# Late attention's scores as products of float32 q and k, without their powers, sums, splits and float16 pairs

## The chip, the cores and the metric

The kernel runs on one core of a Trainium2 chip. The metric is the device time of one execution in microseconds (us), the median of three runs. Engines: PE (matrix products), PEld (its weight loads), DVE and POOL (vector), ACT (scalar), SP (which issues most DMA transfers). The inputs lie in DRAM as float32.

## The reference

Block-local attention over chunks of 64 positions (8 batches, 8 heads, 576 positions, head size 64), then a feed-forward network with `g = h - tanh(h)`:

```python
scores = scale * np.matmul(q_c, k_c.transpose(0, 1, 2, 4, 3))   # scale = 1/8, chunks of 64
scores = scores - np.max(scores, axis=-1, keepdims=True)
attn = np.exp(scores)
attn = attn / (np.sum(attn, axis=-1, keepdims=True) + 1e-09)
out = np.matmul(attn, v_c)
...
h = x @ w_in            # x: 4608 x 512, w_in: 512 x 2048
g = h - np.tanh(h)
return (g @ w_out).astype(np.float32)   # w_out: 2048 x 512
```

## The kernel before

**Groups.** The 4608 tokens are 36 pairs of 128; nine groups have four pairs (512 tokens) each. Groups 0 and 1 are *early*: their attention is in plain float32 (class `Early`, whose `products`, L183, does 16 float32 products of 64x64 a pair) while weights are still being loaded. Groups 2 to 8 are *late* (class `Late`): a group is done in two halves `b` of two pairs, in the shadow of the FFN of the group before. `FAST = 2` is the first of them.

**Late attention before the change.** q, k and v are loaded raw (L303: `xl<-qL`, `rawk<-kL`, `rawv<-vL`). For each of the three a power of two is wanted that brings it into float16's range: sums of magnitudes over a partition (q and k on ACT by `spread`, L107; v as a maximum on DVE in `halves`, L318) go to DRAM and come back on all partitions (`sent`, `returned`: the tiles `hop`, `all`), `greatest` and `scales` make the powers. `split` writes a float16 head on ACT (L341) and a float16 remainder on DVE (L342) for each half of q, k and v. `scores` then takes three terms (head by head, remainder by head, head by remainder), each of them 32 products of 64x64:

```python
for i, (a, b) in enumerate(((0, 0), (1, 0), (0, 1))):
    for e in range(2):
        for hp in range(4):
            for c, u in ((0, 0), (1, 1), (0, 1), (1, 0)):
```

Here `c` chooses the half of the rows and `u` the half of the columns of PE's array. Such a run of products of one line (L353) is called a burst below; the products of the attention's weights with v come in bursts of the same form, and these stay. The powers of q and k go into the scale of the exponential (`d["exp"]`, L370).

**The FFN.** Groups 0 and 1 use class `FeedForward` (first products L534 into PSUM tiles `ph`, activation L546/L543 to `t`, DVE L547/L544, then `gh` on ACT, L554, and `gl` on DVE, L555, second products L565 into `po`), group 0 with float32 weights in two parts (`wh`, `wl`). Groups 2 to 8 use class `Fast` (L617 and L657, all in float16). The first weights become float16 pairs between groups 0 and 1 (`convert`, L455 and L456 on ACT, L457 and L458 on DVE): `most` sums over the weights (L424 to L428 on DVE, then a reduction over partitions on POOL, L430), `power_of_two` (L114 to L116) gives `to_w`, and the first converted weight lies in the tile `first_place`.

**Order.** Up to the end of the first group's FFN a part of the work is put in order by the scheduler from the code's order and its own costs. From `with tc.manual_schedule()` on, the order is that of the code: `ahead` puts each step of late attention into a numbered slot of the FFN loop (16 units a group, two slots a unit). At the boundary between the two, the loads of group 2 and what comes just ahead of the manual part (`sums` of k, `halves` of v) are still placed by the scheduler, among the manual steps too. All DMA issues named here stand in SP's queue and are issued in its order.

Of the kernel before, what the change touches and what calls it, by code (L numbers as in the profile page):

```python
# [57 lines left out]
def attn_ffn_kernel(ctx: ExitStack, tc: tile.TileContext, qE, kE, vE, qL, kL, vL, w_in, w_out, out):  # L58
# [99 lines left out]
    class Early:  # L158
# [110 lines left out]
    class Late:  # L269
# [4 lines left out]
        def __init__(self, pool):  # L274
            self.pool, self.st = pool, defaultdict(dict)

            self.raw = {n: xpool.tile([P, KC, MOST], F32R, name="xl").bitcast(F32) if n == "q" else pool.tile([P, MOST // P, H * CH], F32, name=f"raw{n}", bufs=1) for n in "qkv"}
            self.q16 = self.v16 = None
            self.hop = ctx.enter_context(tc.tile_pool(name="hop", bufs=2, space=bass.MemoryType.DRAM))

        def sent(self, g):

            d = self.st[f"g{g}"]
            d["hop"] = self.hop.tile([P, 3], F32, name="hop")
            nc.sync.dma_start(out=d["hop"], in_=d["sums"])

        def returned(self, g):

            d = self.st[f"g{g}"]
            d["all"] = self.pool.tile([P, P, 3], F32, name="all", bufs=1)  # L290
            nc.sync.dma_start(out=d["all"].rearrange("p n c -> p (n c)"), in_=d["hop"].rearrange("p c -> (p c)").unsqueeze(0).broadcast_to([P, 3 * P]))

        def greatest(self, g):

            d = self.st[f"g{g}"]
            most = self.pool.tile([P, 3], F32, name="most", bufs=2)
            nc.vector.reduce_max(out=most, in_=d["all"].rearrange("p n c -> p c n"), axis=AX.X)
            self.scales(g, most)

        def load(self, p, i, some="qkv"):  # L300
# [4 lines left out]
        def sums(self, g, n, other):  # L305

            d = self.st[f"g{g}"]
            if "sums" not in d:
                d["sums"] = self.pool.tile([P, 3], F32, name="sums", bufs=2)
            spread(other.bitcast(U8).rearrange("p (a n) -> p a n", n=H * CH), self.raw[n], d["sums"][:, "qkv".index(n):"qkv".index(n) + 1])  # L310

        def halves(self, g, i):

            d = self.st[f"g{g}"]
            if i == 0:
                d["v"] = self.pool.tile([P, 2], F32, name="v", bufs=2)
            v = d["v"]
            nc.vector.tensor_reduce(out=v[:, i:i + 1], in_=self.raw["v"][:, 2 * i:2 * i + 2].rearrange("p i n -> p (i n)"), axis=AX.X, op=ALU.max, apply_absolute_value=True)  # L318
            if i:
                nc.vector.tensor_scalar(out=d["sums"][:, 2:3], in0=v[:, 0:1], scalar1=v[:, 1:2], scalar2=2.0 ** -12, op0=ALU.max, op1=ALU.mult)  # L320

        def scales(self, g, top):

            d = self.st[f"g{g}"]
            d["to"], d["from"] = (self.pool.tile([P, 3], F32, name=m, bufs=2) for m in ("to", "from"))
            power_of_two(top, d["to"], d["from"])
            d["exp"] = self.pool.tile([P, 1], F32, name="exp", bufs=2)
            nc.vector.scalar_tensor_tensor(out=d["exp"], in0=d["from"][:, 0:1], scalar=scale, in1=d["from"][:, 1:2], op0=ALU.mult, op1=ALU.mult)
            from_x[g], to_x[g] = d["from"][:, 2:3], d["to"][:, 2:3]

        def split(self, g, b, n):

            d, to = self.st[g, b], self.st[f"g{g}"]["to"][:, "qkv".index(n):"qkv".index(n) + 1]
            d["exp"] = self.st[f"g{g}"]["exp"]
            raw = self.raw[n][:, 2 * b:2 * b + 2].rearrange("p e n -> p (e n)")
            if n == "k":
                t = self.pool.tile([P, 2, 2 * H * CH], F16, name="a", bufs=1)
                hl = d["k"] = t[:, 0], t[:, 1]
            else:
                hl = self.q16 if n == "q" else self.v16  # L340
            nc.scalar.activation(hl[0], raw, AF.Copy, scale=to)  # L341
            nc.vector.scalar_tensor_tensor(out=hl[1], in0=raw, scalar=to, in1=hl[0], op0=ALU.mult, op1=ALU.subtract)  # L342

        def products(self, ps, stationary, moving):


            for i, (a, b) in enumerate(((0, 0), (1, 0), (0, 1))):
                for e in range(2):
                    for hp in range(4):
                        for c, u in ((0, 0), (1, 1), (0, 1), (1, 0)):  # L350
                            r = slice(c * CH, (c + 1) * CH)
                            first = i == e == hp == 0
                            nc.tensor.matmul(ps(c, e, hp)[u * D:(u + 1) * D], lhsT=stationary(a, r, e, hp, u), rhs=moving(b, r, e, hp, u), start=first, stop=(i == 2), skip_group_check=True)  # L353

        def scores(self, g, b):
            d = self.st[g, b]
            ps = d["ps"] = ps_a.tile([P, 2, 2, 4, CH], F32, name="psa")
            q, k = ([t.rearrange("p (e hp u n) -> p e hp u n", e=2, hp=4, u=2) for t in hl] for hl in (self.q16, d["k"]))
            self.products(lambda c, e, hp: ps[:, c, e, hp], lambda a, r, e, hp, u: q[a][r, e, hp, u], lambda b, r, e, hp, u: k[b][r, e, hp, u])

        def shifted(self, g, b):
            d = self.st[g, b]
# [4 lines left out]

        def exponent(self, g, b):
            d = self.st[g, b]
            nc.scalar.activation(d["s"], d["s"], AF.Exp, scale=d["exp"])  # L370

        def totals(self, g, b):
            d = self.st[g, b]
# [23 lines left out]
        def values(self, g, b, x):  # L397
            d = self.st.pop((g, b))
            xh, xl = x
            ps = ps_a.tile([P, 2, 4, 2, CH], F32, name="psa")  # L400
            v = [t.rearrange("p (e hp u n) -> p e hp u n", e=2, hp=4, u=2) for t in self.v16]
            self.products(lambda c, e, hp: ps[:, c, hp, e], lambda a, r, e, hp, u: v[a][r, e, hp, u], lambda b, r, e, hp, u: d["a16"][b][r, e, hp, u])
# [357 lines left out]
            store(nc.sync, 1, right)  # L760
            store(nc.scalar, 0, left)

    def sums(att, g, n):
        att.sums(g, n, ffn.tile([P, MOST], F32, name="t", bufs=3))

    def ahead(att, at, g):

        o = 2 * FC * (g - FAST)
# [2 lines left out]
            at[o + 2 * unit + part].append(lambda: f(*args))  # L771

        late = g == FAST
        later = g == FAST + 1
        put(1 + later, 0, sums, att, g, "q")
        if not late:
            put(2 + later, 0, sums, att, g, "k")
            put(0 if later else -3, later, att.halves, g, 0)
            put(2, not later, att.halves, g, 1)
        put(1 if late else 4, late, att.sent, g)  # L780
        put(2 if late else 4, not late, att.returned, g)
        put(4 if late else 5, -0.5 if late else 1, att.greatest, g)
        put(14 if late else 9, 1, lambda: powers.update({g: half.power_of(g)}))
        put(6, 0, lambda: xs.update({g: new_half_x()}))
        for b, u in enumerate((3, 13) if late else (6, 14)):
            put(u + late, -0.5 if late else 1, att.split, g, b, "q")
            spaced = late and not b
            put(u + 1 + spaced, -0.5 if spaced else 0, att.split, g, b, "k")
            other = u + 3 if spaced else u + 2 if late else u + 1
            put(other, -0.5 if spaced else 1, att.split, g, b, "v")  # L790
            if g + 1 < NG:
                for i in (2 * b, 2 * b + 1):
                    put(u + 1 + spaced, 1, att.load, FIRST[g + 1] + i, i, "qk")
                    put(other, 1, att.load, FIRST[g + 1] + i, i, "v")
            u += late
            put(u + 2, 0, att.scores, g, b)
# [174 lines left out]
        return [place_of("l", 0, fc, dtype) for fc in ORDER[some]]  # L971

    def for_attention():
        att.q16, att.v16 = places(slice(0, 2)), places(slice(2, 4))

    at[2].append(lambda: half.powers(1))
    def convert(i):
# [100 lines left out]
```

## Time and profile before

| | |
|---|---|
| time, median of 3 runs | 791.15 us (791.11 to 792.21) |
| span of the profiled execution | 789.5 us |
| PE busy | 780.6 us, 99% |
| DVE, ACT, POOL busy | 629.4, 467.7, 410.2 us |
| granted clock of PE, 216 to 776 us | 1.00 |

The time is measured around the whole execution, the span from its first to its last recorded instruction; the median lies 1.65 us above the span. The busy shares are averages over all stages. Line numbers in the rows are those of the kernel before.

### The profile page before, as it was taken

How to read it: one execution, taken by the hardware profiler on the slowest of the kernel's cores; microseconds unless marked ns; L12 is line 12 of the kernel's file. 1: busy time of each engine (PE TensorE's matmuls, PEld its weight loads, DVE VectorE, ACT ScalarE, POOL GpSimd, SP SyncE). 2: the span in 40 equal slices, each digit the busy share in tenths (PEclk: the TensorE clock that was granted, in tenths of full speed). 3: DMA queues.
4: the chain of work that ended last, by engine and by line, in shares of the span. 5: the costliest groups of instructions: out<-in, count | busy, mean ns of one | idle time of the engine just before them, and what ended most of it. 6: DMA issues, size and time to landing. Idle time of an engine off the chain costs nothing.

```text
span 789.5 us, 21247 instructions
## 1 busy us (share of the span) xinstructions
PE 780.6 (99%) x9096; PEld 658.7 (83%) x9099; DVE 629.4 (80%) x856; ACT 467.7 (59%) x714; POOL 410.2 (52%) x461
## 2 busy tenths in 40 slices
PE   8999999999999999999999999999999999999997
PEld 4878875666788888888888888888888888888887
DVE  5896998899899787878878687968796878686554
ACT  6887999667586456544654565546454645454332
POOL 1100003398876656565657456656556565656462
PEclk9999999999999999999999999999999999999999
DMA  9854442210232223222422132222322230302000
GB/s 349 320 188 159 161 161 63 81 28 15 67 91 83 54 82 60 87 54 59 78 43 90 30 98 48 82 49 74 65 83 56 81 64 3 54 2 54 2 27 27
DMA packets 61054, 64.62 MB, mean 82 GB/s; under 512 B 33952, under 2 KB 42016, under 8 KB 60960
## 3 DMA queue, kind: packets, MB, share of 16 engines
q1 hardware_dynamic: 60528, 62.61, 27.8%
q8 instruction: 71, 1.16, 0.6%
q10 hardware_dynamic: 432, 0.66, 0.2%
q14 instruction: 23, 0.19, 0.1%
HBM read 46.47 MB, written 9.45 MB: 71 GB/s over the span
## 4 chain that ended last, share of the span: by engine, by line
PE 94%; DVE 2%; DMA 1%; ACT 1%; issue 0%; POOL 0%; POOLq 0%; SPq 0%; ACTq 0%
PE ph L617 37%; PE po L657 32%; PE po L565 10%; PE ph L534 9%; PE psa L353 3%; PE po L732 1%; DMA raw<-w_out 1%; PE psa L183 1%; DMA k<-kE 1%; DVE wl L148 0%; PE psa L244 0%; ACT w L133 0%; ACT s L218 0%; DVE w L141 0%; DVE w L137 0%
## 5 line engine op out<-in xcount | busy, mean ns | idle before, releaser
L617 PE MATMUL ph<-xh,wh 128*128 128x256 f16 x2520 | 291.1, 273 | 0.0
L617 PEld LDWEIGHTS <-wh 128*128 128x128 f16 x2520 | 245.4, 98 | 29.2 <-issue 0.5
L626 POOL TENSOR_TENSOR xl<-xl 128x256 f32<-128x256 f32 x111 | 112.6, 1015 | 222.7 <-DVE xl L625 222.0
L624 ACT ACTIVATE t<-ph,sig 128x512 f32<-128x512 f32 x112 | 77.0, 687 | 216.2 <-PE ph L617 214.6
L625 DVE SCALAR_TENSOR_TENSOR xl<-ph,sig,t 128x512 f32<-128x512 f32 x112 | 83.5, 745 | 78.9 <-ACT t L624 78.8
L657 PEld LDWEIGHTS <-wl 128*128 128x128 f16 x1134 | 110.9, 98 | 12.9
L628 POOL TENSOR_TENSOR xl<-xl 128x256 f32<-128x256 f32 x111 | 103.9, 936 | 0.0
L627 POOL TENSOR_TENSOR xl<-xl 128x128 f32<-128x128 f32 x111 | 101.4, 913 | 0.0
L657 PE MATMUL po<-wl,wl 128*128 128x256 f16 x648 | 101.0, 273 | 0.0
L638 DVE SCALAR_TENSOR_TENSOR gl<-xl,to_g,gh 128x896 f16<-128x896 f32 x56 | 82.9, 1481 | 7.9 <-ACT gh L637 7.9
L657 PE MATMUL po<-wh,wl 128*128 128x256 f16 x486 | 85.5, 273 | 0.0
L638 DVE SCALAR_TENSOR_TENSOR wl<-xl,to_g,wl 128x896 f16<-128x896 f32 x56 | 71.1, 1269 | 16.6 <-ACT wl L637 15.1
L657 PEld LDWEIGHTS <-gh 128*128 128x128 f16 x756 | 73.0, 98 | 8.8
L637 ACT ACTIVATE wl<-xl,to_g 128x896 f16<-128x896 f32 x56 | 57.9, 1035 | 32.4 <-POOL xl L628 31.5
L657 PE MATMUL po<-wl,gh 128*128 128x256 f16 x544 | 74.7, 273 | 0.0
L534 PE MATMUL ph<-xh,wh 128*128 128x512 f16 (+2 forms) x252 | 59.3, 377 | 0.4 <-ACT xh L266 0.3
L637 ACT ACTIVATE gh<-xl,to_g 128x896 f16<-128x896 f32 x56 | 57.8, 1032 | 1.3 <-DVE from L115 0.6
L565 PE MATMUL po<-wh,gh 128*128 128x512 f32 x128 | 52.9, 416 | 0.0
L565 PE MATMUL po<-wl,gh 128*128 128x512 f32 x128 | 50.3, 395 | 0.2 <-POOL wl L148 0.2
L657 PE MATMUL po<-wl,gl 128*128 128x256 f16 x272 | 42.9, 273 | 0.0
L657 PEld LDWEIGHTS <-gl 128*128 128x128 f16 x378 | 37.0, 98 | 4.3
L657 PE MATMUL po<-wh,gh 128*128 128x256 f16 x212 | 36.3, 273 | 0.0
(185 smaller groups left out, 1236.9 us busy)
## 6 DMA issues: line engine op xcount, KB each, us to landing
raw<-w_in SPq DMA_DIRECT2D x16, 512.0 KB, 3.7
raw<-w_out SPq DMA_DIRECT2D x16, 512.0 KB, 5.1
xl<-qL SPq DMA_DIRECT2D x28, 256.0 KB, 3.2
rawk<-kL SPq DMA_DIRECT2D x28, 256.0 KB, 3.3
rawv<-vL SPq DMA_DIRECT2D x28, 256.0 KB, 3.4
out<-wl SPq DMA_DIRECT2D x55, 128.0 KB, 1.8
q<-qE SPq DMA_DIRECT2D x8, 256.0 KB, 5.7
v<-vE SPq DMA_DIRECT2D x8, 256.0 KB, 6.1
```

The costliest lines, as they stand in the source:

```text
L353: nc.tensor.matmul(ps(c, e, hp)[u * D:(u + 1) * D], lhsT=stationary(a, r, e, hp, u), rhs=moving(b, r, e, hp, u), start=first, stop=(i == 2 ...
L534: nc.tensor.matmul(ph, lhsT=w[:, kc * P:(kc + 1) * P], rhs=x[b][:, kc, cols], start=(k == 0), stop=(k == 3 * KC - 1))
L565: nc.tensor.matmul(self.po[t], lhsT=gg[a][:, ts], rhs=wt[fc][1][b], start=(fc == 0 and a == b == 0), stop=(fc == FC - 1 and a == 1))
L617: nc.tensor.matmul(self.ph[:, 1 - f::2, :], lhsT=half_w[fc][:, w, kc * P:(kc + 1) * P], rhs=rhs, start=(k == 0), stop=(k == 3 * KC - 1))
L624: nc.scalar.activation(t, self.ph, AF.Tanh, scale=sig)
L625: nc.vector.scalar_tensor_tensor(out=u[:, :4], in0=self.ph, scalar=sig, in1=t, op0=ALU.mult, op1=ALU.subtract)
L626: engine.tensor_add(u[:, 4:6], u[:, 1:3], u[:, 0:4:3])
L627: engine.tensor_add(u[:, 6], u[:, 1], u[:, 2])
L628: engine.tensor_sub(u[:, 0:4:3], u[:, 0:2], u[:, 2:4])
L637: nc.scalar.activation(gh, u, AF.Copy, scale=powers[1])
L638: nc.vector.scalar_tensor_tensor(out=gl, in0=u, scalar=powers[1], in1=gh, op0=ALU.mult, op1=ALU.subtract)
L657: nc.tensor.matmul(place[m], lhsT=part[:, self.SUM[m]], rhs=w[m][:, o], start=first, stop=(last and part is gl), skip_group_check=True)
```

## The change

The scores of late attention multiply q and k in float32, straight from the tiles into which they were loaded: one term of 32 products instead of three of 32. The sums and powers of q and k, their splits and their float16 places go. v keeps its power and its float16 pair; the hop through DRAM has one column. The steps of a group are put into other slots, the loads of q and k behind the scores that read the same tiles, and the first late group's loads are issued in the order v, k, q.

```diff
         def scales(self, g, top):
-            d = self.st[f"g{g}"]
-            d["to"], d["from"] = (self.pool.tile([P, 3], F32, name=m, bufs=2) for m in ("to", "from"))
-            power_of_two(top, d["to"], d["from"])
-            d["exp"] = self.pool.tile([P, 1], F32, name="exp", bufs=2)
-            nc.vector.scalar_tensor_tensor(out=d["exp"], in0=d["from"][:, 0:1], scalar=scale, in1=d["from"][:, 1:2], op0=ALU.mult, op1=ALU.mult)
-            from_x[g], to_x[g] = d["from"][:, 2:3], d["to"][:, 2:3]
...
+            to_x[g], from_x[g] = (self.pool.tile([P, 1], F32, name=m, bufs=2) for m in ("to", "from"))
+            power_of_two(top, to_x[g], from_x[g])
+
+        def split(self, g, b):
+
+            raw = self.raw["v"][:, 2 * b:2 * b + 2].rearrange("p e n -> p (e n)")
+            hi, lo = self.v16
+            nc.scalar.activation(hi, raw, AF.Copy, scale=to_x[g])
+            nc.vector.scalar_tensor_tensor(out=lo, in0=raw, scalar=to_x[g], in1=hi, op0=ALU.mult, op1=ALU.subtract)
+
+        def products(self, ps, stationary, moving, terms):
+
+
+            for i, (a, b) in enumerate(terms):
                 for e in range(2):
                     for hp in range(4):
                         for c, u in ((0, 0), (1, 1), (0, 1), (1, 0)):
                             r = slice(c * CH, (c + 1) * CH)
-                            first = i == e == hp == 0
-                            nc.tensor.matmul(ps(c, e, hp)[u * D:(u + 1) * D], lhsT=stationary(a, r, e, hp, u), rhs=moving(b, r, e, hp, u), start=first, stop=(i == 2), skip_group_check=True)
+                            first = len(terms) == 1 or i == e == hp == 0
+                            nc.tensor.matmul(ps(c, e, hp)[u * D:(u + 1) * D], lhsT=stationary(a, r, e, hp, u), rhs=moving(b, r, e, hp, u), start=first, stop=(i == len(terms) - 1), skip_group_check=True)
 
         def scores(self, g, b):
             d = self.st[g, b]
             ps = d["ps"] = ps_a.tile([P, 2, 2, 4, CH], F32, name="psa")
-            q, k = ([t.rearrange("p (e hp u n) -> p e hp u n", e=2, hp=4, u=2) for t in hl] for hl in (self.q16, d["k"]))
-            self.products(lambda c, e, hp: ps[:, c, e, hp], lambda a, r, e, hp, u: q[a][r, e, hp, u], lambda b, r, e, hp, u: k[b][r, e, hp, u])
+            q, k = (self.raw[n][:, 2 * b:2 * b + 2].rearrange("p e (hp u n) -> p e hp u n", hp=4, u=2) for n in "qk")
+            self.products(lambda c, e, hp: ps[:, c, e, hp], lambda a, r, e, hp, u: q[r, e, hp, u], lambda b, r, e, hp, u: k[r, e, hp, u], ((0, 0),))
...
-            nc.scalar.activation(d["s"], d["s"], AF.Exp, scale=d["exp"])
+            nc.scalar.activation(d["s"], d["s"], AF.Exp, scale=scale)
...
         late = g == FAST
-        later = g == FAST + 1
-        put(1 + later, 0, sums, att, g, "q")
         if not late:
-            put(2 + later, 0, sums, att, g, "k")
-            put(0 if later else -3, later, att.halves, g, 0)
-            put(2, not later, att.halves, g, 1)
-        put(1 if late else 4, late, att.sent, g)
-        put(2 if late else 4, not late, att.returned, g)
+            put(-3, 0, att.halves, g, 0)
+            put(1, 1, att.halves, g, 1)
+        put(1 if late else 2, late, att.sent, g)
+        put(2, not late, att.returned, g)
...
                 for i in (2 * b, 2 * b + 1):
-                    put(u + 1 + spaced, 1, att.load, FIRST[g + 1] + i, i, "qk")
+                    put(u + late + 2, 1, att.load, FIRST[g + 1] + i, i, "qk")
                     put(other, 1, att.load, FIRST[g + 1] + i, i, "v")
...
-    for n in "kvq":
+    for n in "vkq":
         for i in range(SIZES[FAST]):
             att.load(FIRST[FAST] + i, i, n)
-    sums(att, FAST, "k")
     for i in range(2):
         att.halves(FAST, i)
     with tc.manual_schedule():
```

The late products with v now pass their three terms as an argument; their code is otherwise the same. In the changed kernel's listings the line numbers are smaller by some 16: L353 is L337 there, L534 L518, L547 L531, L555 L539, L554 L538, L565 L549, L318 L312, L427 L411, L455 L439, L456 L440.

Three places of the instruction order show what moves. The first is DVE's queue at the boundary, where the sums over the first weights (`sums_102`) become `to_w`. Before, it reads:

```order
L547 TENSOR_TENSOR t<-ph,t 128x512
L426 TENSOR_SCALAR sums_102<-sums_102 128x16
L427 TENSOR_REDUCE most_1521<-sums_102 128x1
L428 TENSOR_SCALAR most_1521<-most_1521 128x1
L114 TENSOR_SCALAR from_w<-top_1527 128x1
L115 TENSOR_SCALAR from_w<-from_w 128x1
L116 RECIPROCAL to_w<-from_w 128x1
```

And after the change, at the same place:

```order
L531 TENSOR_TENSOR t<-ph,t 128x512
L312 TENSOR_REDUCE v<-rawv 128x1
L410 TENSOR_SCALAR sums_102<-sums_102 128x16
L539 TENSOR_TENSOR gl<-t,gh 128x512
L312 TENSOR_REDUCE v<-rawv 128x1
L411 TENSOR_REDUCE most_1519<-sums_102 128x1
L314 TENSOR_SCALAR sums<-v 128x1
L412 TENSOR_SCALAR most_1519<-most_1519 128x1
L114 TENSOR_SCALAR from_w<-top_1525 128x1
L115 TENSOR_SCALAR from_w<-from_w 128x1
L116 RECIPROCAL to_w<-from_w 128x1
```

The two reductions over v's halves and `gl` moved ahead of `to_w`; before, all three stand behind it.

The second place is PE's queue a little later: the last twelve second products of group 0's FFN (those with `wh_1089`) and the first products of group 1 with `first_place`. Before:

```order
L565 MATMUL po_515<-wh_1085,gl 128x512
L534 LDWEIGHTS first_place
L534 MATMUL ph<-xh,first_place 128x512
L534 LDWEIGHTS first_place
L534 MATMUL ph<-xh,first_place 128x512
L534 LDWEIGHTS first_place
L534 MATMUL ph<-xh,first_place 128x512
L534 LDWEIGHTS first_place
L534 MATMUL ph<-xh,first_place 128x512
L534 LDWEIGHTS first_place
L534 MATMUL ph<-xh,first_place 128x512
L565 MATMUL po_113<-wh_1089,gh 128x512
```

After:

```order
L549 MATMUL po_515<-wh_1085,gl 128x512
L518 LDWEIGHTS first_place
L518 MATMUL ph<-xh,first_place 128x512
L549 MATMUL po_113<-wh_1089,gh 128x512
L549 MATMUL po_113<-wl_1090,gh 128x512
```

Four of the five products with `first_place` moved behind the twelve. On ACT, between `first_place` and the `gh` that these twelve read, the changed order is this:

```order
L439 ACTIVATE first_place<-wh_70,to_w 128x512
L530 ACTIVATE t<-ph 128x512
L440 ACTIVATE first_place<-wl_71,to_w 128x512
L439 ACTIVATE wh_1542<-wh_1059,to_w 128x512
L538 CAST gh<-t 128x512
```

So four conversions and activations stand between `to_w` and that `gh`; before, `to_w` was there long ahead of it.

## Rows read from the trace of the kernel before

**Rows 1.** The page: span, and part 1, each engine's busy us.
```profile
span 789.5 us, 21247 instructions
PE 780.6 (99%) x9096; PEld 658.7 (83%) x9099; DVE 629.4 (80%) x856; ACT 467.7 (59%) x714; POOL 410.2 (52%) x461
```
**Rows 2.** Windows: stretch, PE, PEld, DVE, ACT, POOL busy; clock, DMA share, GB/s.
```profile
216.00:776.00 560.00, 560.00 (x7300) 498.85 (x7299) 436.83 (x541) 299.61 (x382) 336.67 (x373) 1.00 0.24 58
```
**Rows 3.** Timeline of PE around a late score burst: start, busy us, work.
```profile
284.58 1.47 PE L617 MATMUL ph<-xh,first_place 128*128 128x256 f16 x12
285.89 1.47 PE L617 MATMUL ph<-xh,wh 128*128 128x256 f16 x12
287.29 0.98 PE L353 MATMUL psa<-a,wl 64*64 64x64 f16 x96
288.20 0.61 PE L657 MATMUL po<-wh,gh 128*128 128x256 f16 x4
```
**Rows 4.** The tile view of `psa`: ns min/median/max, first and last start.
```profile
L353 PE MATMUL psa<-a,wl x1344: 192/193/213, 149.9 to 701.3; 64*64 64x64 f16 x192
```
**Rows 5.** Timeline of PE around an early score burst.
```profile
32.74 1.16 PE L183 MATMUL psa<-k,q 64*64 64x64 f32 x64
33.84 0.97 PE L534 MATMUL ph<-xh,wh 128*128 128x512 f32 x3
```
**Rows 6.** Timeline of PE: another early score burst.
```profile
52.23 1.63 PE L183 MATMUL psa<-k,q 64*64 64x64 f32 x64
```
**Rows 7.** Groups by line and form: busy us, mean ns, idle before.
```profile
L342 DVE SCALAR_TENSOR_TENSOR a<-rawk,to,a 128x1024 f16<-128x1024 f32 x14 | 20.6, 1469 | 0.4 <-ACT a L341 0.4
L342 DVE SCALAR_TENSOR_TENSOR wl<-xl,to,wl 128x1024 f16<-128x1024 f32 x14 | 18.5, 1322 | 1.4 <-ACT wl L341 1.4
L107 ACT ACTIVATE t<-rawk 128x2048 uint8<-128x2048 f32 x7 | 13.3, 1900 | 0.0
```
**Rows 8.** Tile view of `rawk`, 106 to 108.1 us: SP's issues, their landing.
```profile
L303 SPq DMA_DIRECT2D rawk<-kL x4: 365/430/432, 106.3 to 107.7; - x4
...
DMA to landing us min/median/max: 4.0/4.3/4.6
```
**Rows 9.** Timeline of DVE at the boundary.
```profile
110.12 0.69 DVE L547 TENSOR_TENSOR t<-ph,t 128x512 f32<-128x512 f32 x1
...
111.13 0.15 DVE L428 TENSOR_SCALAR most<-most 128x1 f32<-128x1 f32 x1
...
112.25 0.16 DVE L116 RECIPROCAL to_w<-from_w 128x1 f32<-128x1 f32 x1
...
114.20 1.21 DVE L318 TENSOR_REDUCE v<-rawv 128x1 f32<-128x1024 f32 x1
115.33 0.41 DVE L458 TENSOR_TENSOR first_place<-first_place,wl 128x512 f16<-128x512 f16 x1
```
**Rows 10.** Timeline of ACT at the boundary.
```profile
112.50 0.71 ACT L455 ACTIVATE first_place<-wh,to_w 128x512 f16<-128x512 f32 x1
...
115.56 0.58 ACT L546 ACTIVATE t<-ph 128x512 f32<-128x512 f32 x1
116.04 1.90 ACT L107 ACTIVATE t<-rawk 128x2048 uint8<-128x2048 f32 x1
...
117.93 0.61 ACT L554 CAST gh<-t 128x512 fp32r<-128x512 f32 x1
```
**Rows 11.** Timeline of PE at the boundary.
```profile
117.45 1.25 PE L534 MATMUL ph<-xh,first_place 128*128 128x512 f16 x5
118.59 0.50 PE L565 MATMUL po<-wh,gh 128*128 128x512 f32 x1
```
**Rows 12.** Timelines of PE and ACT around 130 us.
```profile
130.01 1.07 PE L565 MATMUL po<-wh,gl 128*128 128x512 f32 x4
131.12 1.24 PE L534 MATMUL ph<-xh,wh 128*128 128x512 f16 x5
...
127.88 1.90 ACT L107 ACTIVATE t<-xl 128x2048 uint8<-128x2048 f32 x1
```

More of the change, by code (lines that the diff above doesn't have):

```diff
@@ L277, in __init__ @@
             self.raw = {n: xpool.tile([P, KC, MOST], F32R, name="xl").bitcast(F32) if n == "q" else pool.tile([P, MOST // P, H * CH], F32, name=f"raw{n}", bufs=1) for n in "qkv"}
-            self.q16 = self.v16 = None
+            self.v16 = None
             self.hop = ctx.enter_context(tc.tile_pool(name="hop", bufs=2, space=bass.MemoryType.DRAM))
@@ L283, in sent @@
             d = self.st[f"g{g}"]
-            d["hop"] = self.hop.tile([P, 3], F32, name="hop")
+            d["hop"] = self.hop.tile([P, 1], F32, name="hop")
             nc.sync.dma_start(out=d["hop"], in_=d["sums"])
@@ L289, in returned @@
             d = self.st[f"g{g}"]
-            d["all"] = self.pool.tile([P, P, 3], F32, name="all", bufs=1)
-            nc.sync.dma_start(out=d["all"].rearrange("p n c -> p (n c)"), in_=d["hop"].rearrange("p c -> (p c)").unsqueeze(0).broadcast_to([P, 3 * P]))
+            d["all"] = self.pool.tile([P, P], F32, name="all", bufs=1)
+            nc.sync.dma_start(out=d["all"], in_=d["hop"].rearrange("p c -> (p c)").unsqueeze(0).broadcast_to([P, P]))
         def greatest(self, g):
             d = self.st[f"g{g}"]
-            most = self.pool.tile([P, 3], F32, name="most", bufs=2)
-            nc.vector.reduce_max(out=most, in_=d["all"].rearrange("p n c -> p c n"), axis=AX.X)
+            most = self.pool.tile([P, 1], F32, name="most", bufs=2)
+            nc.vector.reduce_max(out=most, in_=d["all"], axis=AX.X)
             self.scales(g, most)
@@ L303, in load @@
                 nc.sync.dma_start(out=self.raw[n][:, i], in_=src[p - NE])
-        def sums(self, g, n, other):
-            d = self.st[f"g{g}"]
-            if "sums" not in d:
-                d["sums"] = self.pool.tile([P, 3], F32, name="sums", bufs=2)
-            spread(other.bitcast(U8).rearrange("p (a n) -> p a n", n=H * CH), self.raw[n], d["sums"][:, "qkv".index(n):"qkv".index(n) + 1])
         def halves(self, g, i):
@@ L316, in halves @@
                 d["v"] = self.pool.tile([P, 2], F32, name="v", bufs=2)
+                d["sums"] = self.pool.tile([P, 1], F32, name="sums", bufs=2)
             v = d["v"]
@@ L319, in halves @@
             if i:
-                nc.vector.tensor_scalar(out=d["sums"][:, 2:3], in0=v[:, 0:1], scalar1=v[:, 1:2], scalar2=2.0 ** -12, op0=ALU.max, op1=ALU.mult)
+                nc.vector.tensor_scalar(out=d["sums"], in0=v[:, 0:1], scalar1=v[:, 1:2], scalar2=2.0 ** -12, op0=ALU.max, op1=ALU.mult)
         def scales(self, g, top):
-            d = self.st[f"g{g}"]
-            d["to"], d["from"] = (self.pool.tile([P, 3], F32, name=m, bufs=2) for m in ("to", "from"))
-            power_of_two(top, d["to"], d["from"])
-            d["exp"] = self.pool.tile([P, 1], F32, name="exp", bufs=2)
-            nc.vector.scalar_tensor_tensor(out=d["exp"], in0=d["from"][:, 0:1], scalar=scale, in1=d["from"][:, 1:2], op0=ALU.mult, op1=ALU.mult)
-            from_x[g], to_x[g] = d["from"][:, 2:3], d["to"][:, 2:3]
[L331 to L347, printed above, removed]
+            to_x[g], from_x[g] = (self.pool.tile([P, 1], F32, name=m, bufs=2) for m in ("to", "from"))
[7 more added lines that the diff above has]
+            for i, (a, b) in enumerate(terms):
                 for e in range(2):
@@ L401, in values @@
             v = [t.rearrange("p (e hp u n) -> p e hp u n", e=2, hp=4, u=2) for t in self.v16]
-            self.products(lambda c, e, hp: ps[:, c, hp, e], lambda a, r, e, hp, u: v[a][r, e, hp, u], lambda b, r, e, hp, u: d["a16"][b][r, e, hp, u])
+            self.products(lambda c, e, hp: ps[:, c, hp, e], lambda a, r, e, hp, u: v[a][r, e, hp, u], lambda b, r, e, hp, u: d["a16"][b][r, e, hp, u], ((0, 0), (1, 0), (0, 1)))
             both = [(slice((2 * b + c) * P, (2 * b + c + 1) * P), ps[:, c].rearrange("p hp e q -> p hp (e q)")) for c in range(2)]
@@ L761, in ending @@
             store(nc.scalar, 0, left)
-    def sums(att, g, n):
-        att.sums(g, n, ffn.tile([P, MOST], F32, name="t", bufs=3))
     def ahead(att, at, g):
@@ L785, in ahead @@
         for b, u in enumerate((3, 13) if late else (6, 14)):
-            put(u + late, -0.5 if late else 1, att.split, g, b, "q")
             spaced = late and not b
-            put(u + 1 + spaced, -0.5 if spaced else 0, att.split, g, b, "k")
             other = u + 3 if spaced else u + 2 if late else u + 1
-            put(other, -0.5 if spaced else 1, att.split, g, b, "v")
+            put(other, -0.5 if spaced else 1, att.split, g, b)
             if g + 1 < NG:
                 for i in (2 * b, 2 * b + 1):
-                    put(u + 1 + spaced, 1, att.load, FIRST[g + 1] + i, i, "qk")
+                    put(u + late + 2, 1, att.load, FIRST[g + 1] + i, i, "qk")
                     put(other, 1, att.load, FIRST[g + 1] + i, i, "v")
@@ L973, in for_attention @@
     def for_attention():
-        att.q16, att.v16 = places(slice(0, 2)), places(slice(2, 4))
+        att.v16 = places(slice(2, 4))
     at[2].append(lambda: half.powers(1))
```

## The prediction

> **What bounds the kernel now.** The page comes first, for the engine that hardly rests: PE is busy for 780.6 of the 789.5 us of the span, DVE and ACT far less [rows 1]. That is an average over stages, so the next view is the table of windows over the late stage, from 216 to 776 us: PE is busy for all of its 560.00 us at a granted clock of 1.00 (the upper level, 2.4 GHz), DVE for 437, ACT for 300, SP's transfers for a quarter of the DMA engines [rows 2]. The view of PE's waits from 75 us on lists nothing. A busy count can hide small pauses, since ends of matmuls are modelled, so the third view is PE's timeline around one score burst: the twelve FFN products ahead of it start 1.31 us / 12 = 0.109 us apart, and the burst of 96 float16 products takes 0.91 us from its first start at 287.29 to the next row's at 288.20 [rows 3]. So in the late stage the end is set by how long PE needs for its own work. DVE, ACT or DMA work that goes away there buys nothing; PE work that comes or goes counts at full price.
>
> **The change part by part.** *The scores.* Each of 7 late groups has two halves, so 14 bursts; the trace has 1344 = 14 x 96 such products [rows 4]. A burst of 96 float16 products becomes 32 products of float32 operands. No product of late attention in the trace reads float32, but the early groups' do, on the same 64x64 tiles: a burst there is 64 records, two for each of 32 products, in the order (0,0), (1,1), (0,1), (1,0) of row half and column half that the changed code issues too. That burst takes 33.84 - 32.74 = 1.10 us to the next row [rows 5], against 0.91 us. The difference is 0.19 us, and 14 x 0.19 = **+2.7 us**. The early burst stands among float32 FFN products and the late one among float16 ones, so I bound the unknown price: from below by the price of a float16 record, 0.91 / 96 = 9.5 ns, times 64 = 0.61 us (-0.30 a burst, -4.2 us in all), from above by the early burst whose row halves don't overlap, 1.63 us of busy time against 1.16 [rows 6], which is 0.47 more (+0.66 a burst, +9.2 us). I take 1.10, the row with the same type, tile and order.
>
> The Trainium skill, page "FP8 and Floating Point Precision", section "TensorE Precision Notes", says that a true float32 product takes four passes through the array. By an estimate from that page, 128 passes in place of 96, a burst would take 0.91 x 128 / 96 = 1.21 us, and the scores would add 4.2 us. No row here shows four passes: the trace has two records for a float32 product, and the sum goes by their 1.10 us.
>
> *What goes.* For q and k: two DVE remainders a half (14 of 1469 ns and 14 of 1322 ns, 39 us in all), two ACT conversions and two ACT sums, of which k's 7 take 13.3 us [rows 7]. From 216 us on all of it lies beside a PE that never stops, so it is worth 0. The hop through DRAM shrinks from three columns to one, and its steps come earlier; q's and k's next loads move behind the scores that still read the raw tiles. SP then waits for PE's score burst with the loads queued behind it; they are wanted a group (some 80 us) later, and transfers fill a quarter of the DMA engines [rows 2]. I cost it at 0; without that cover a load's landing of 4 to 5 us [rows 8] would stand once in a group.
>
> *The boundary before the late stage.* Here the order changes, and PE has little slack. Before, DVE reads the sums of the first weights at 110 us, POOL reduces them over the partitions, and DVE's reciprocal gives `to_w` at 112.25 + 0.16 = 112.41 [rows 9]; ACT scales `first_place` with it at 112.50 [rows 10]. The two reductions of v's halves come behind it, from 114.20 [rows 9]. After the change v's loads stand where k's stood, issued from 106.3 us on and landing 4.0 to 4.6 us later [rows 8], and the order puts both reductions ahead of that chain. The first needs the second load (issued at about 106.8): it starts at about 111.2. It holds DVE for 115.33 - 114.20 = 1.13 us [rows 9] (112.3); a small step and `gl` (0.69 us as the operation of its kind at 110.12 [rows 9]) bring 113.1, the second reduction 114.3, two more small ones 114.5. From the start of L428 to the end of L116 is 112.41 - 111.13 = 1.28 us [rows 9]: `to_w` at about 115.8, 3.4 us later than before.
>
> ACT's order then is `first_place` (first part), `t`, `first_place` (second), the next weight's first part, and only then `gh`, which PE wants: conversions of 0.71 us and `t` of 0.58 that overlap by some 0.1 us (115.56 to 116.04 for one of 0.58 [rows 10]). So 0.6 + 0.5 + 0.6 + 0.6 = 2.3 us after 115.85, `gh` starts at about 118.15 and is there at 118.75. Before it was there at 117.93 + 0.61 = 118.54 [rows 10], while PE did five products of the next group with `first_place` from 117.45 on and began the last twelve products on `gh` at 118.59 [rows 11]. Now only one of the five stands ahead of the twelve: PE is through with it at 117.45 + 0.23 = 117.68 and waits until about 118.8, 0.2 us later than 118.59, with four products of (118.59 - 117.45) / 5 = 0.23 us still to do. That is 0.2 + 0.9 = **+1.1 us**. Its bounds: 0, if `to_w` comes 1.1 us sooner than I reckon; 1.9, if each of the eight steps of this chain comes 0.1 us later.
>
> *A stall that goes.* At 130.01 four products of the float32 FFN start; the next row starts 1.11 us later, 0.2 more than such a row needs (4 x 0.23). PE waits for a PSUM tile that DVE frees after ACT's `gh`, which stood behind the sum over q at 127.88, 1.90 us [rows 12]. That sum is gone: **-0.2 us** (bounds -0.2 and 0).
>
> *The sum.* 789.5 + 2.7 + 1.1 - 0.2 = 793.1 us of span. The runs' median of 791.15 is 1.65 us above the profiled span, so the time is 793.1 + 1.65 = **794.7 us**.
>
> **The rivals.** (a) *The boundary costs nothing*: `gh` comes in time, or the other products fill the gap; 789.5 + 2.7 - 0.2 + 1.65 = 793.6. For it: the chain has eight steps, each good to 0.1 us; against it: it would need 1.1 us. (b) *Float32 among float16 is dearer*, so that a float32 product costs four float16 ones: 32 x 4 x 9.5 ns = 1.21 us a burst, 14 x 0.30 = 4.2 instead of 2.7, 796.3. For it: no row shows such a burst among float16 products; against it: the early row [rows 5]. It is what the four passes of the Trainium skill's page "FP8 and Floating Point Precision" would make. (c) *The bursts run two wide*, as in the row of 1.63 us: +9.2, 801.2. That happened where the scheduler pulled the halves apart; the late stage is issued in the written order. (d) *Faster: the price is by record, not by pass.* 64 records instead of 96 at 9.5 ns: 14 x -0.30 = -4.2, with the boundary's 0.9, 787.9. It decides as soon as a burst of 64 records costs less than 0.91 - 2.5 / 14 = 0.73 us; the early row's 1.10 speaks against it. The Trainium skill's page "TensorE: Matmul & The Clock Gate", Part 1, "Wait — 56ns, not 53.3ns?", leans this way: starts of matmuls are never closer than about 25 ns, so 32 starts fewer would save an estimated 0.8 us a burst, 11 us in all. The trace does not bear that floor out for these tiles: 96 starts in 0.91 us [rows 3]. (e) *No change*: the freed 39 us of DVE and the ACT work end small pauses inside PE's stream that its busy count hides, and give back 2 to 3 us: 792. Against it: the FFN products start 0.109 us apart right up to the burst [rows 3].
>
> **How the numbers follow.** The forecast has 0.64 (own range 793.9 to 795.5), (a) 0.14, (b) 0.09, (c) 0.03, (d) 0.05, (e) 0.05. Predicted time 794.7. The range reaches down over (a) and up to (b): 792.8 to 796.3, which leaves out (c), (d), (e) and some tails. About 0.2% (1.6 us) is what a measurement here can tell from no change: faster is (d), 0.05; within it (e), 0.05; slower all the rest, 0.90.
>
> **What the changed profile would show.** Score bursts as one row of 64 records of float32, 64x64, the next row 1.10 us later (right), 1.2 (b), 1.57 (c), 0.6 (d). PE still busy for all of 216 to 776. `first_place` scaled on ACT at 115.8; one product with it ahead of the last twelve, which start at 118.8; `to_w` before 114.7 would make the boundary free. No gap at 130.9. DVE and ACT lose their q and k work with no gain on PE. Wrong it would be by another price of the burst above all: 0.1 us there moves the time by 1.4 us.

## The result and the profile after

The changed kernel takes 796.57 us (median of 4 runs, 795.91 to 797.63) against 791.68 us of the runs of before beside it: ratio 1.0065, 95% interval 1.0051 to 1.0079. It is slower, as forecast, but by 4.9 us (5.4 against the 791.15 from which the forecast was made) instead of 3.5, and its time lies just above the range (796.3). The page of the profiled execution (796.24 us) answers to [rows 1]:

```profile
span 794.4 us, 20238 instructions
PE 783.6 (99%) x8651; PEld 660.9 (83%) x8651; DVE 587.7 (74%) x821; ACT 411.1 (52%) x658; POOL 404.9 (51%) x461
```

DVE lost 42 us of work and ACT 57, PE gained 3, and the span 4.9. The windows over the stage of [rows 2] show that PE's work is not all of it:

```profile
216.00:776.00 560.00, 559.09 (x6882) 497.56 (x6881) 403.82 (x510) 250.88 (x334) 334.67 (x371) 1.00 0.22 57
```

PE now rests 0.91 us in a stage in which it did not rest before. The view of PE's waits from 75 us on, empty before, names it (columns: us waited, times, longest):

```profile
PE ph L601 <- DVE xl L609: 0.9, 1, 0.9
PE po L549 <- ACT gh L538: 0.7, 1, 0.7
```

The second wait is the one forecast at the boundary, the first was not forecast. Now each term in turn.

**The bursts.** The timeline of PE around the burst of [rows 3]:

```profile
288.75 1.47 PE L601 MATMUL ph<-xh,wh 128*128 128x256 f16 x12
290.15 1.16 PE L337 MATMUL psa<-rawk,xl 64*64 64x64 f32 x64
291.25 0.61 PE L641 MATMUL po<-wh,gh 128*128 128x256 f16 x4
```

1.10 us, as in the early stage [rows 5] and as predicted: 0.19 more than before, 14 x 0.19 = 2.7 us. All 14 bursts of the trace take 1.09 to 1.10 us; unrounded the difference is 0.185 us a burst, 2.6 us in all.

**The boundary.** PE's timeline of the changed kernel, answering to [rows 11]:

```profile
118.01 0.39 PE L518 MATMUL ph<-xh,first_place 128*128 128x512 f16 x1
119.13 0.50 PE L549 MATMUL po<-wh,gh 128*128 128x512 f32 x1 [0.73 <-ACT gh L538]
...
121.98 2.55 PE L518 MATMUL ph<-xh,first_place 128*128 128x512 f16 x11
124.37 5.34 PE L518 MATMUL ph<-xh,wh 128*128 128x512 f16 x24
```

and DVE and ACT there, answering to [rows 9, 10]:

```profile
111.61 1.22 DVE L312 TENSOR_REDUCE v<-rawv 128x1 f32<-128x1024 f32 x1 [0.24 <-DMA rawv<-vL]
...
113.45 1.22 DVE L312 TENSOR_REDUCE v<-rawv 128x1 f32<-128x1024 f32 x1
...
115.94 0.16 DVE L116 RECIPROCAL to_w<-from_w 128x1 f32<-128x1 f32 x1
```

```profile
116.14 0.72 ACT L439 ACTIVATE first_place<-wh,to_w 128x512 f16<-128x512 f32 x1 [1.48 <-DVE to_w L116]
...
118.47 0.60 ACT L538 CAST gh<-t 128x512 fp32r<-128x512 f32 x1
```

It goes as written: the reductions first, `to_w` at 116.10, `gh` at 119.07, PE waiting with one product done. Before, the row of 24 products that follows began here:

```profile
122.97 5.34 PE L534 MATMUL ph<-xh,wh 128*128 128x512 f16 x24
```

From the first product with `first_place` to that row it was 122.97 - 117.45 = 5.52 us and is now 124.37 - 118.01 = 6.36: 0.84 us lost, where 1.1 was forecast.

**The stall that goes.** Around 130 us [rows 12] the four products are followed 0.92 us later, no longer 1.11; the 0.2 us came back:

```profile
131.40 1.08 PE L549 MATMUL po<-wh,gl 128*128 128x512 f32 x4
132.32 1.90 PE L518 MATMUL ph<-xh,wh 128*128 128x512 f16 x8
```

**The wait nobody forecast.** At the start of group 2's FFN, where 72 products stood without a pause before, there is now one of 0.91 us. PE before, then PE after:

```profile
215.05 8.03 PE L617 MATMUL ph<-xh,wh 128*128 128x256 f16 x72
222.92 1.69 PE L657 MATMUL po<-wl,gh 128*128 128x256 f16 x14
```

```profile
216.65 5.41 PE L601 MATMUL ph<-xh,wh 128*128 128x256 f16 x48
222.98 2.78 PE L601 MATMUL ph<-xh,wh 128*128 128x256 f16 x24 [0.91 <-DVE xl L609]
225.59 1.69 PE L641 MATMUL po<-wl,gh 128*128 128x256 f16 x14
```

From the first of the 72 to the row behind them it was 7.87 us and is 8.94: 1.07 us lost. PE waits for the PSUM tile `ph`, which DVE's subtraction `xl<-ph` frees. DVE before, then DVE after:

```profile
218.55 0.74 DVE L503 SCALAR_TENSOR_TENSOR wl<-wh,to_w,wl 128x512 f16<-128x512 f32 x1
219.21 0.74 DVE L625 SCALAR_TENSOR_TENSOR xl<-ph,sig,t 128x512 f32<-128x512 f32 x1
...
222.07 1.21 DVE L318 TENSOR_REDUCE v<-rawv 128x1 f32<-128x1024 f32 x1
```

```profile
220.15 1.21 DVE L312 TENSOR_REDUCE v<-rawv 128x1 f32<-128x1024 f32 x1
221.39 0.21 DVE L314 TENSOR_SCALAR sums<-v 128x1 f32<-128x1 f32 x1
221.52 0.74 DVE L487 SCALAR_TENSOR_TENSOR wl<-wh,to_w,wl 128x512 f16<-128x512 f32 x1
222.18 0.75 DVE L609 SCALAR_TENSOR_TENSOR xl<-ph,sig,t 128x512 f32<-128x512 f32 x1
```

Group 3's second reduction over v stood behind that subtraction and now stands ahead of it, 221.52 - 220.15 = 1.37 us of DVE. Before, `ph` was free at 219.95 and wanted at about 215.05 + 48 x 0.109 = 220.28: a margin of 0.33 us, in a stage where DVE is idle for a fifth of the time (busy 436.83 of 560 us [rows 2]).

**The sum.** 2.6 (bursts, 0.185 each) + 0.84 - 0.19 + 1.07 = 4.3 us. The span grew by 4.9; the other 0.56 us arise before the change acts (118.01 against 117.45 at the first product with `first_place`; up to about 111 us the instructions of DVE, ACT and POOL stand in the same order in both traces, and PE waits for nothing from there to that product). The runs below show that this moves from run to run.

### The profile page after: what moved, and what is told of

Same layout as the page of the kernel before. It is cut to its first block, busy times and chain, and to the rows that moved or that the text cites. A ratio compares the mean times of both kernels' runs of the same rounds, so it can differ in the third digit from the quotient of the medians.

```text
span 794.4 us, 20238 instructions
## 1 busy us (share of the span) xinstructions
PE 783.6 (99%) x8651; PEld 660.9 (83%) x8651; DVE 587.7 (74%) x821; ACT 411.1 (52%) x658; POOL 404.9 (51%) x461
## 4 chain that ended last, share of the span: by engine, by line
PE 92%; DVE 4%; ACT 2%; issue 1%; DMA 0%; POOLq 0%; POOL 0%; ACTq 0%; SPq 0%
PE ph L601 36%; PE po L641 31%; PE po L549 9%; PE ph L518 9%; PE psa L337 4%; PE psa L183 1%; PE ph L846 1%; PE po L716 1%; ACT s L218 1%; DVE w L141 1%; DMA raw<-w_in 0%; ACT w L133 0%; DVE wl L148 0%; DVE v L312 0%; DVE w L137 0%
## 5 line engine op out<-in xcount | busy, mean ns | idle before, releaser
L610 POOL TENSOR_TENSOR xl<-xl 128x256 f32<-128x256 f32 x111 | 103.2, 930 | 228.6 <-DVE xl L609 227.5
L611 POOL TENSOR_TENSOR xl<-xl 128x128 f32<-128x128 f32 x111 | 109.3, 985 | 0.0
L612 POOL TENSOR_TENSOR xl<-xl 128x256 f32<-128x256 f32 x111 | 104.5, 941 | 0.0
L622 DVE SCALAR_TENSOR_TENSOR wl<-xl,to_g,wl 128x896 f16<-128x896 f32 x56 | 76.5, 1366 | 19.1 <-ACT wl L621 18.9
L518 PE MATMUL ph<-xh,wh 128*128 128x512 f16 (+2 forms) x252 | 59.3, 377 | 0.3 <-ACT xh L266 0.3
L549 PE MATMUL po<-wh,gh 128*128 128x512 f32 x128 | 52.9, 416 | 0.7 <-ACT gh L538 0.7
L549 PE MATMUL po<-wl,gh 128*128 128x512 f32 x128 | 50.2, 395 | 0.2 <-POOL wl L148 0.2
```

Source lines behind the costliest of these rows:

```text
L518: nc.tensor.matmul(ph, lhsT=w[:, kc * P:(kc + 1) * P], rhs=x[b][:, kc, cols], start=(k == 0), stop=(k == 3 * KC - 1))
L549: nc.tensor.matmul(self.po[t], lhsT=gg[a][:, ts], rhs=wt[fc][1][b], start=(fc == 0 and a == b == 0), stop=(fc == FC - 1 and a == 1))
L610: engine.tensor_add(u[:, 4:6], u[:, 1:3], u[:, 0:4:3])
L611: engine.tensor_add(u[:, 6], u[:, 1], u[:, 2])
L612: engine.tensor_sub(u[:, 0:4:3], u[:, 0:2], u[:, 2:4])
L622: nc.vector.scalar_tensor_tensor(out=gl, in0=u, scalar=powers[1], in1=gh, op0=ALU.mult, op1=ALU.subtract)
```

## The experiments

The early stage differs between profiled executions by up to 3 us, so beside each time the table has the stretch from the start of the first row with `first_place` on PE (117 to 120 us) to the end of the span, which takes this away. Before, it is 789.5 - 117.45 = 672.1 us, after it is 794.4 - 118.01 = 676.4.

| run | median, us | ratio to before (95%) | span | first row with `first_place` | rest | against before |
|---|---|---|---|---|---|---|
| changed kernel | 796.57 | 1.0065 (1.0051 to 1.0079) | 794.4 | 118.01 | 676.4 | +4.3 |
| e1, group 3's reductions back | 795.58 | 1.0050 (1.0038 to 1.0063) | 796.3 | 120.05 | 676.2 | +4.1 |
| e2, boundary back | 795.38 | 1.0043 (1.0031 to 1.0055) | 792.9 | 117.26 | 675.6 | +3.5 |
| e3, both back | 794.65 | 1.0036 (1.0024 to 1.0048) | 794.0 | 119.52 | 674.5 | +2.4 |
| e4, scores alone | 793.93 | 1.0033 (1.0021 to 1.0045) | 793.4 | 118.82 | 674.6 | +2.5 |
| e5, two float16 terms | 787.58 | 0.9949 (0.9935 to 0.9963) | 785.6 | 117.21 | 668.4 | -3.7 |
| e7, row halves apart | 806.62 | 1.0190 (1.0175 to 1.0206) | 804.4 | 117.41 | 687.0 | +14.9 |
| e8, early half in before | 792.81 | 1.0012 (1.0003 to 1.0020) | 791.3 | 118.12 | 673.2 | +1.1 |
| e9, boundary in before | 794.87 | 1.0040 (1.0027 to 1.0053) | 791.8 | 117.12 | 674.7 | +2.6 |
| e10, one float16 term | 784.62 | 0.9910 (0.9894 to 0.9927) | 782.8 | 118.20 | 664.6 | -7.5 |
| e11, two terms, no remainder of k | 787.64 | 0.9950 (0.9936 to 0.9965) | 787.3 | 118.98 | 668.3 | -3.8 |

A part of what the rest takes away is the clock. In the executions of e1, e3, e4 and e11, which reach that row last (118.82 to 120.05 us), the granted clock was 0.91 to 0.95 from 20 to 40 us, a mean of the levels 1.2 and 2.4 GHz. In the others it was 1.00, and the row starts at 117.12 to 118.20. From 10 to 20 us PE was busy for 6.0 to 6.8 us in those four and for 6.6 to 7.7 in the others. What makes the 1.1 us between the others is open.

**e1, e2 and e3: undo the two moves of v's reductions.** The edit of e1 in `ahead`, and that of e2; e3 has both.

```diff
-            put(-3, 0, att.halves, g, 0)
-            put(1, 1, att.halves, g, 1)
+            later = g == FAST + 1
+            put(0 if later else -3, later, att.halves, g, 0)
+            put(2 if later else 1, not later, att.halves, g, 1)
```

```diff
-    for i in range(2):
-        att.halves(FAST, i)
     with tc.manual_schedule():
...
         for i in range(AHEAD):
             convert(i)
+            if i < 2:
+                att.halves(FAST, i)
```

> The changed kernel, with one thing undone: group 3's two reductions over v's halves stand again in the slots that they had before (the second one behind the division of group 2's second half, not ahead of the FFN's subtraction that frees PE's PSUM tile). Nothing is left out of the computation. Theory: in the changed kernel PE waited 0.91 us at 222.07 us because DVE did this reduction (1.21 us, with a small step 1.37 us from start to start) ahead of the subtraction; with it behind, the wait goes, PE starts that row some 1.1 us sooner, and the span falls from 794.4 to 793.3 us (ratio to before about 1.005). Rival: the wait has another cause, such as the exponentials or the hop coming at other times; then the row still waits 0.9 us and the span stays at 794.4.

> The changed kernel, with one thing undone: group 2's two reductions over v's halves are written behind the first two weight conversions, so that they stand behind to_w in DVE's queue again, as before; the loads keep the order v, k, q. Nothing is left out. Theory: to_w is back at about 112.4 to 113 us, five products with first_place stand again ahead of the last twelve second products, PE does not wait for gh, and the 0.8 us that PE lost there come back: span 793.6 us, with the wait at 222 us still there (0.9 us). Rival: the loss at the boundary came with the order of the loads or with jitter of the early stage; then the span stays at 794.4.

> Both of the other two edits at once. Nothing is left out. Theory: what stays is the price of the float32 bursts, 14 x 0.185 = 2.6 us, less the 0.2 us of the stall at 130.9 that went: span 789.5 + 2.6 - 0.2 = 791.9 us, ratio to before about 1.003. Rival (a third cause in the late stage, unseen): 793 us or more.

In e1 the wait that group 3's reduction made is gone and the 72 products stand together again (the first line is from PE's timeline); only the boundary's wait is left in the view of PE's waits (the second):

```profile
219.54 8.03 PE L601 MATMUL ph<-xh,wh 128*128 128x256 f16 x72
...
PE po L549 <- ACT gh L538: 1.5, 1, 1.5
```

That one has grown, so that the span of this execution, 796.3 us, tells nothing by itself; four of e1's five other runs have 793.3 to 793.9 us, beside the 793.3 expected. The program there is that of the changed kernel; what differs is when v landed (4.7 to 5.2 us after its issue in e1, 4.0 to 4.2 in the changed kernel's execution), as DVE shows:

```profile
114.50 1.22 DVE L312 TENSOR_REDUCE v<-rawv 128x1 f32<-128x1024 f32 x1 [1.09 <-DMA rawv<-vL]
```

So the boundary's price is not fixed: it hangs on a transfer. From the first product with `first_place` to the row of 24 the loss is 0.84 us in the changed kernel's execution, 0.99 in e7's, where v landed 4.1 to 4.7 us after its issue, and 127.27 - 120.05 - 5.52 = 1.70 in e1's. e2 is the counterpart: five products with `first_place` in a row again (PE's timeline), and only the other wait left, unchanged (the view of PE's waits):

```profile
117.26 1.25 PE L518 MATMUL ph<-xh,first_place 128*128 128x512 f16 x5
...
PE ph L601 <- DVE xl L609: 0.9, 1, 0.9
```

Its rest is 0.8 us below the changed kernel's, as expected. In e3 the view is empty, and the rest is 2.4 us above that of before: the bursts less the 0.2 us. Its span, 794.0, is above the 793 that I had set for the rival, but its first row with `first_place` starts 2.07 us later than before (119.52 against 117.45); without that it is 791.9, as expected. The rivals (another cause of the wait, jitter, a third cause) fall: each move carries its own wait, and in the rest no third cause of more than some 0.1 us is left. The medians agree, with wider intervals: the changed kernel's lies 1.9 us above e3's, and 0.84 + 1.07 = 1.91.

**e4: the scores alone.** The kernel before with the new `scores`, the constant scale in the exponential and the loads of q and k behind the scores; powers, sums and splits of q and k stay.

```diff
-            self.products(lambda c, e, hp: ps[:, c, e, hp], lambda a, r, e, hp, u: q[a][r, e, hp, u], lambda b, r, e, hp, u: k[b][r, e, hp, u])
+            self.products(lambda c, e, hp: ps[:, c, e, hp], lambda a, r, e, hp, u: q[r, e, hp, u], lambda b, r, e, hp, u: k[r, e, hp, u], ((0, 0),))
...
-                    put(u + 1 + spaced, 1, att.load, FIRST[g + 1] + i, i, "qk")
+                    put(u + late + 2, 1, att.load, FIRST[g + 1] + i, i, "qk")
```

> The kernel before, with only the scores changed: 32 float32 products of raw q and k a burst and a constant scale in the exponential, the loads of q and k behind them; the sums, powers and splits of q and k are still made, and nobody reads the float16 pairs. Theory: the 14 bursts alone cost 14 x 0.185 = 2.6 us, the boundary and group 3 stay as before: span 792.1 us, ratio 1.0033. Rival (the split work that the change takes off DVE and ACT was holding PE up, or the loads behind the scores cost something): the span differs from 792.1 by more than 0.5 us.

The rest grows by 2.5 us; PE has no wait (the span, 793.4, holds a start that is 1.37 us later than before). With or without the removed DVE and ACT work (e4 against e3, 674.6 and 674.5) the rest is the same to 0.1 us, and the stall alone tells them apart: behind the four products of [rows 12] the next row starts 1.11 us later in e4, which keeps the sums, and 0.91 in e3. So the work that the change takes away is worth those 0.2 us and nothing else. By the medians e3 lies 0.7 us above e4, which their intervals allow.

**e8 and e9: the two moves in the kernel before.** In e8 group 3's second reduction goes to unit 1 (with the tile `sums` made a step earlier), in e9 the first late group's loads go out in the order v, k, q.

```diff
-            put(2, not later, att.halves, g, 1)
+            put(1 if later else 2, 1, att.halves, g, 1)
```

```diff
-    for n in "kvq":
+    for n in "vkq":
```

> The kernel before with one thing moved: group 3's second reduction over v's halves stands in the slot that the changed kernel gives it, ahead of the FFN's subtraction, and all the rest as before. Nothing is left out. Theory: DVE frees the PSUM tile 1.37 us later, PE waits there for about 1.0 us, span 790.6 us (ratio 1.0014). Rival (the wait needs other parts of the change): no wait, 789.5.

> The kernel before with one thing changed: the first late group's loads are issued in the order v, k, q. The scheduler then puts both reductions over v's halves ahead of to_w on DVE, as in the changed kernel, but four, not one, of the five products with first_place stay ahead of the last twelve second products. Nothing is left out. Theory: to_w comes 3.4 us later and gh about 0.2 to 1 us later than before, of which PE loses that and one product's 0.22 us: 0.4 to 1.2 us between the first product with first_place and the 24 products that follow the twelve. Rival: no loss there (under 0.1 us).

e8 brings the wait into the kernel before, alone, at the same size, and 1.1 us:

```profile
PE ph L619 <- DVE xl L627: 0.9, 1, 0.9
```

e9 costs 2.6 us of the rest, more than twice what I expected at most. The order of the loads is enough to bring the wait for `gh`, but two more come behind it:

```profile
PE po L565 <- ACT gh L554: 1.2, 1, 1.2
PE ph L534 <- DVE t L544: 1.0, 1, 1.0
PE ph L534 <- DVE gl L555: 0.2, 1, 0.2
```

I had counted only the first. The last is the stall at 130 us that the kernel before has too [rows 12]. For the second, the sum over q is not the cause: it starts on ACT at 130.16 us, behind that wait, which ends at 127.71. The sum over k (1.90 us from 116.78) stands on ACT ahead of `gh` and of the second part of `first_place`, where the changed kernel has weight conversions; that it sets the second wait is likely and was not tried.

**e5, e10, e11 and e7: what a burst costs.** e5 and e10 leave terms out of the kernel before (their scores carry less of q's and k's precision; e10 makes no remainders of q and k either), e11 is e5 without k's remainder, e7 orders the float32 products of the changed kernel by row half. The edits, cut to what differs in the scores (in e5, e10 and e11 `products` takes the terms as an argument): first e5 and e11, then e10, then e7.

```diff
-            self.products(lambda c, e, hp: ps[:, c, e, hp], lambda a, r, e, hp, u: q[a][r, e, hp, u], lambda b, r, e, hp, u: k[b][r, e, hp, u])
+            self.products(lambda c, e, hp: ps[:, c, e, hp], lambda a, r, e, hp, u: q[a][r, e, hp, u], lambda b, r, e, hp, u: k[b][r, e, hp, u], ((0, 0), (1, 0)))
```

```diff
-            self.products(lambda c, e, hp: ps[:, c, e, hp], lambda a, r, e, hp, u: q[a][r, e, hp, u], lambda b, r, e, hp, u: k[b][r, e, hp, u])
+            self.products(lambda c, e, hp: ps[:, c, e, hp], lambda a, r, e, hp, u: q[a][r, e, hp, u], lambda b, r, e, hp, u: k[b][r, e, hp, u], ((0, 0),))
```

```diff
-                for e in range(2):
+                for c0, e in ((0, 0), (0, 1), (1, 0), (1, 1)) if len(terms) == 1 else ((None, 0), (None, 1)):
                     for hp in range(4):
-                        for c, u in ((0, 0), (1, 1), (0, 1), (1, 0)):
+                        for c, u in ((0, 0), (1, 1), (0, 1), (1, 0)) if c0 is None else ((c0, 0), (c0, 1)):
```

> The kernel before with two of the three float16 terms in the scores (the term head by remainder is left out): 64 products of 64x64 in a burst, as many records as the float32 burst has. Theory (a record is paid by what it passes through the array; a float32 record costs about twice a float16 one): the row of 64 takes 0.65 us to the next row (0.91 less 32 records of 8.2 ns), 14 x -0.26 = -3.7 us, span 785.9 us if the early stage is as in the profile of before. Rival (64 records cost the same whatever their type): 1.10 us, span 792.

> The kernel before with one of the three float16 terms in the scores (head by head; both remainders of q and k and their two terms are left out): 32 products of 64x64 in a burst. Theory (8.3 ns for a record at 64 columns of float16, as the step from 96 to 64 products gave: 0.268 us for 32): the burst takes 0.37 us to the next row, 14 x -0.536 = -7.5 us, ratio to before 0.9905. Rival (a floor in a burst's start and end, not its products, sets the price): less than 5 us gained.

> The kernel before with two float16 terms in the scores (the term head by remainder is left out) and without k's remainder, which nobody reads then: 14 DVE instructions of 1.47 us fewer than in the run with two terms that still made it. Theory (DVE's work is hidden behind PE in the late stage): the same time as that run, ratio 0.995, span from the first product with first_place to the end within 0.1 us of that run's. Rival (DVE's work counts): up to 14 x 1.47 us less.

> The changed kernel with the 32 float32 products of a burst in another order: all products of row half 0, then all of row half 1. Nothing is left out. Theory: only two of the array's four quarters work at once, the burst takes 1.57 us to the next row, 0.47 more than 1.10, and the span is 14 x 0.47 = 6.6 us above the changed kernel's. Rival (the long early row of 1.63 us had another cause, such as operands that came late): 1.10 us and no change.

One burst of e5, one of e10 and one of e7, each with the row behind it:

```profile
286.31 0.71 PE L353 MATMUL psa<-a,wl 64*64 64x64 f16 x64
286.95 0.61 PE L657 MATMUL po<-wh,gh 128*128 128x256 f16 x4
```

```profile
286.44 0.45 PE L354 MATMUL psa<-a,wl 64*64 64x64 f16 x32
286.81 0.61 PE L658 MATMUL po<-wh,gh 128*128 128x256 f16 x4
```

```profile
291.89 1.91 PE L337 MATMUL psa<-rawk,xl 64*64 64x64 f32 x64
293.73 0.61 PE L641 MATMUL po<-wh,gh 128*128 128x256 f16 x4
```

0.91, 0.64 and 0.37 us for 96, 64 and 32 float16 products: 8.4 ns each, and 0.10 us once a burst. If a float32 burst has the same 0.10 us, which is not shown, a float32 record costs (1.10 - 0.10) / 64 = 15.6 ns, and a float32 product, two records, 31 ns: 3.7 float16 products. The starts of the single records in the trace give a little less: in the middle of the burst four start every 58 ns, so 29 ns a product, 3.4 float16 ones. At the same count of 64 records float16 takes 0.64 us and float32 1.10, so the rival by which a record has one price falls. The Trainium skill's page "FP8 and Floating Point Precision" (section "TensorE Precision Notes") gives four passes for a true float32 product; the 3.4 to 3.7 lie 7 to 14% below. The page "TensorE: Matmul & The Clock Gate" (Part 1, "Wait — 56ns, not 53.3ns?") has starts never closer than about 25 ns; 8.4 ns a product says otherwise for tiles of 64x64.

e7's burst takes 1.84 us, not 1.57: the direction was right, the size not, and the rival (1.10 us and no change) falls. In the middle of this burst two records start every 58 ns, where the order that mixes the row halves starts four: in 0.29 us (292.20 to 292.49) 18 records are at work on PE, in the changed kernel (290.40 to 290.69) 36. The early row of [rows 6], from which I took 1.57, was only partly apart: 14 records are at work there from 52.59 to 52.88 us and 34 from 53.20 to 53.49. Whether the products themselves or the weight loads between them set the 58 ns was not tried. e11 takes the time of e5: 14 x 1.47 us of DVE work less buys nothing, which the rival had at up to 20 us.

e10 beats both kernels, 784.62 us, by leaving out what the float32 products were to keep: it is 12 us faster than the changed kernel at the price of q and k rounded to float16. It shows where time can be had here, in fewer passes on PE.

## Why the prediction was wrong

- **What bounds the kernel** was right but for one place: PE's own time. Removing 42 us of DVE and 57 us of ACT work gave back the 0.2 us that was named, and no more (e3, e4, e11).
- **The bursts** were right: 2.7 forecast, 2.5 to 2.6 measured, at the price of the early row (e4). The price of rival (c), 1.57 us a burst, was too low: the row of [rows 6] keeps its row halves apart only in part, and e7 has 1.84.
- **The boundary** was right in each step (the reductions first, `to_w` at 115.8 forecast and 116.10 measured, in an execution that was 0.56 us late by then; one product ahead; a wait for `gh`). 1.1 forecast, 0.84 in the profiled execution, more where v lands later (e1).
- **The stall** of 0.2 us went as forecast.
- **The step that failed** is the sentence on what goes: "The hop through DRAM shrinks from three columns to one, and its steps come earlier", which has no term in the sum. The prediction reasons there about work that goes, which "lies beside a PE that never stops", and for steps that stay in the late stage and only move it has no price. With the hop's steps the reductions of `halves` moved too, and I did not follow them in DVE's queue past the subtraction that frees PE's PSUM tile. DVE's busy share there left room for 1.4 us; the place did not, with 0.33 us of margin. That is 1.07 us (e1 and e8 show it from both sides); the sign "PE still busy for all of 216 to 776" failed by it (559.09 of 560.00 us). With these 1.07 us the forecast would have been 795.8, inside the range that I gave.
- **What is left.** With the terms as measured the time is 789.5 + 4.3 + 1.65 = 795.5 us, and 1.1 us are left to the median: 0.56 before the change acts, 0.19 around the span of the profiled execution (796.24 - 794.4 = 1.84 us against 1.65), and 0.33 from that execution to the median. They are of the size by which the early stage and the time around the span differ from run to run (first row with `first_place` at 117.1 to 120.1 us; 797.63 - 794.9 = 2.73 us around the span in another run of the changed kernel). So it took the missed wait and such a difference together to leave the range. No single cause of the difference was shown.

## What to carry to other kernels

An engine that never waits is not an engine with slack around it: where PE runs without a pause, list for every step that is moved what it now stands ahead of on its own engine, and the margin of the row that frees PE's next tile, however idle the engine is on average. And where PE bounds the time, price a change of type by a row of the same type, tile and order: it gave 1.10 us a burst here, as measured, where the count of records gave 0.61 and the count of passes 1.21. The vector work saved was worth next to nothing beside a PE that is the limit.

## What the runs showed of the hardware

- Products of 64x64 on the four quarters of the array cost 8.4 ns each in float16 when their order mixes the quarters, and a burst of them 0.10 us beside (0.91, 0.64, 0.37 us for 96, 64, 32).
- A float32 product of that shape costs 29 to 31 ns, 3.4 to 3.7 float16 ones. Four records start every 58 ns; with the row halves apart it is two, and the same 32 products take 1.84 instead of 1.10 us.
- The early stage varies: the same program reached the same place at 117.1 to 120.1 us, the latest four with a granted clock of 0.91 to 0.95 from 20 to 40 us. At the same place of the same program a load of v landed 4.0 to 5.2 us after its issue (changed kernel, e1, e7).
